# A planner's lengths for VectorE's work and the start of joined blocks, in a retention and feed-forward kernel

## The chip, the cores and the metric

The kernel runs on one core of a Trainium2 chip. The metric is the time of one execution in device microseconds (us). All runs told here were in the fast state or single looks of unknown state; the granted clock of TensorE was 0.997 to 1.0 in every run. Medians are of several runs. A ratio is the mean time of one kernel's fast runs over the mean of the other's fast runs of the same rounds, so it is not quite the ratio of the medians quoted.

## The reference, cut to what matters

Retention (attention with a decay in place of softmax) over 8 batches of 8 heads, 576 positions, head size 64; then a feed-forward layer whose activation is the squared relu. Everything is float32 outside; the kernel works in float16 with float32 sums.

```python
scores = scale * np.matmul(q, k.transpose(0, 1, 3, 2))
Dmat = np.where(rel >= 0, gamma[:, None, None] ** rel[None, :, :], 0.0)
attn = np.matmul(scores * Dmat[None], v)
x = attn.transpose(0, 2, 1, 3).reshape(B * S, H * D)     # 4608 x 512
r = np.maximum(x @ w_in, 0.0)                            # w_in 512 x 2048
out = (r * r) @ w_out                                    # w_out 2048 x 512
```

## The kernel before

The 4608 rows are 36 units of 128 rows, two to a group, 18 groups. A group goes through these steps:

- GpSimd casts k and q to float16 and multiplies v by its decay (units from 8 on); DMA transposes k and q.
- TensorE makes scores and sums of k and v in 64x64 tiles; VectorE masks the scores (rT), updates the states (Rm, stmp, R), and, after TensorE's outputs (psO), scales them into xT.
- TensorE multiplies xT by w_in (ph, first layer). ScalarE takes the relu (rl); the square (gT) is ScalarE's for seven of eight blocks and VectorE's for the last (from group 2 to 15; elsewhere VectorE has more of them).
- From group 2 on the second layer is a Strassen product: seven products in place of eight, for which VectorE first makes four sums and differences (gS), each in two halves. They are S1 to S4; S2 = gT(1,1) - S3 is used by the third product; its second half needs the last square, and S1, S4 follow.

The order on each engine isn't written by hand. Every piece is a task with an engine, a priority, a planned length in us and dependences. A list scheduler plays them through once, while the program is built, and each engine's instructions are emitted in the order so found:

```python
class Schedule:
    def add(self, eng, key, dur, fn, deps=(), acq=(), ...): ...
    def emit(self):
        ...        # at each moment each idle engine takes the ready task with the lowest key
        push(now + t["dur"], "end", t)
        ...
        for t in order:
            t["fn"]()
```

The chip then runs each engine's list in that order, waiting where a semaphore says so. A planned length that is wrong costs nothing in itself; it can put an instruction of TensorE ahead of something that isn't ready.

The other thing that the change touches is the joining. A group that isn't joined has a block fa (scores and sums) and later a block fb (outputs, in two parts with an explicit drain instruction of TensorE between). From group JOIN on, the outputs of a group and the scores and sums of the next are issued together, in f1 and f2, with no drain:

```python
def joined(g):
    return JOIN <= g < last_g
...
    def f1():
        emit_out1(g)
        emit_scores(g + 1)
    def f2():
        emit_sums(g + 1, "prS")
        emit_out2(g)
    ...                      # masks after f1; xT of g and the states of g + 1 after f2
else:
    def fb():
        emit_out1(g)
        nc.tensor.drain()
        emit_out2(g)
```

After f2, VectorE's keys put the first unit's xT, then the three state steps of the next group's first unit, then the second unit's xT. The next group's first layer needs both xT.

## Time and profile before

| | |
|---|---|
| time, median of 3 runs | 294.85 us (294.26 to 295.28) |
| the profiled execution | span 293.8 us, in a run of 295.6 us |
| TensorE busy | 284.2 us of the span |
| VectorE, ScalarE, GpSimd busy | 197.1, 188.0, 88.5 us |

The pages and lists that carry the argument stand in the prediction. One more view belongs beside them: busy time by engine in two stretches, where the column after the stretch is its length, then each engine's busy us and its count of instructions.

```profile
100.00:125.00 25.00, 23.46 (x420) 19.89 (x418) 18.88 (x37) 17.12 (x32) 8.49 (x10) 1.00 0.88 185
125.00:145.00 20.00, 19.19 (x291) 16.65 (x290) 14.22 (x29) 12.19 (x24) 8.66 (x11) 1.00 0.94 199
```

The order of the columns is TensorE matmul, TensorE weight load, VectorE, ScalarE, GpSimd. TensorE, busy nearly everywhere else, is idle for 1.54 us of the first stretch and 0.81 of the second.

### The profile page before, as it was taken

To read this page: it belongs to the slowest core of one execution; us is meant where nothing else is said; L and a number is where in the kernel's file an instruction comes from. 1 tells how busy PE (TensorE), PEld (TensorE's weight loads), DVE (VectorE), ACT (ScalarE), POOL (GpSimd) and SP (SyncE) were. 2 spreads that over 40 slices of the span, in tenths; PEclk is the share of its full clock that TensorE was granted. 3 is DMA by queue.
4 is the path that set the end of the run, shared out by engine and by line. 5 is a ranking of instruction groups with operands and counts; after the bars stand their busy time and mean duration, and the time that the engine had idled before them with its cause. 6 is when DMAs were issued, how large, how long until landed. Compare 5 with 4: busy or idle time off the path is not lost.

```text
span 293.8 us, 10069 instructions
## 1 busy us (share of the span) xinstructions
PE 284.2 (97%) x4328; PEld 234.0 (80%) x4328; DVE 197.1 (67%) x430; ACT 188.0 (64%) x354; POOL 88.5 (30%) x123
## 2 busy tenths in 40 slices
PE   8989999999999998999899999999999999999995
PEld 3548755688888877888788888888888888888884
DVE  3796579759484877757776867657796776564732
ACT  5457875386748665657576666766766576757830
POOL 4343364433343425151604142615150500000000
PEclk9999999999999999999999999999999999999999
DMA  7999999999989999797859599999796920201004
GB/s 201 327 370 386 366 286 266 217 230 191 232 203 194 183 198 199 177 201 184 179 144 211 139 199 208 204 212 184 187 192 163 165 74 2 74 3 71 2 0 145
DMA packets 139421, 54.14 MB, mean 184 GB/s; under 512 B 118128, under 2 KB 130928, under 8 KB 139376
## 3 DMA queue, kind: packets, MB, share of 16 engines
q1 hardware_dynamic: 139072, 53.23, 80.3%
q8 instruction: 34, 0.56, 0.9%
q10 hardware_dynamic: 304, 0.26, 0.3%
q14 instruction: 11, 0.09, 0.1%
HBM read 36.70 MB, written 9.44 MB: 157 GB/s over the span
## 4 chain that ended last, share of the span: by engine, by line
PE 85%; DVE 9%; ACT 3%; issue 1%; DVEq 0%
PE ph L827 38%; PE po L916 31%; PE po L865 5%; PE psO L343 4%; PE warm L247 3%; DVE gS L893 2%; PE psS L343 2%; PE psc L343 2%; PE psT L418 1%; ACT gT L845 1%; ACT rl L835 1%; DVE gT L847 1%; DVE xT L704 1%; DVE rx L461 1%; DVE vx L399 1%
## 5 line engine op out<-in xcount | busy, mean ns | idle before, releaser
L827 PE MATMUL ph<-xT,w_in 128*128 128x256 f16 x1152 | 138.3, 273 | 1.0 <-DVE xT L704 1.0
L827 PEld LDWEIGHTS <-w_in 128*128 128x128 f16 x1152 | 111.0, 98 | 15.8 <-DVE xT L704 1.2
L835 ACT ACTIVATE rl<-ph 128x512 f16<-128x512 f32 x144 | 84.2, 588 | 47.8 <-PE ph L827 44.0
L845 ACT ACTIVATE gT<-rl 128x512 f16<-128x512 f16 x104 | 65.6, 631 | 3.1
L916 PEld LDWEIGHTS <-gS 128*128 128x128 f16 x512 | 49.1, 98 | 8.4 <-DVE gS L893 2.3
L916 PE MATMUL po<-wT,gS 128*128 128x256 f16 x384 | 52.0, 273 | 1.5 <-DVE gS L893 1.5
L893 DVE TENSOR_TENSOR gS<-gT,gS 128x512 f16<-128x512 f16 x64 | 35.5, 556 | 13.3 <-ACT gT L845 12.7
L893 DVE TENSOR_TENSOR gS<-gT 128x512 f16<-128x512 f16 x64 | 31.2, 488 | 14.8 <-ACT gT L845 14.7
L916 PEld LDWEIGHTS <-gT 128*128 128x128 f16 x384 | 37.1, 98 | 4.5
L355 POOL CAST kq<-k 128x512 f16<-128x512 f32 x28 | 18.6, 666 | 63.2 <-DMA k<-in_k_dram 61.4
L916 PE MATMUL po<-w_out,gT 128*128 128x256 f16 x256 | 34.5, 273 | 0.0
L367 POOL TENSOR_TENSOR v<-v,vdec_full 128x512 f16<-128x512 f32 x24 | 26.0, 1084 | 20.4 <-DMA v<-in_v_dram 14.0
L847 DVE TENSOR_TENSOR gT<-rl 128x512 f16<-128x512 f16 x40 | 20.4, 509 | 15.3 <-ACT rl L835 15.0
L929 ACT COPY u<-po 128x256 f32<-128x256 f32 x32 | 11.9, 371 | 25.0 <-PE po L916 24.8
L355 POOL CAST kq<-q 128x512 f16<-128x512 f32 x28 | 18.7, 669 | 28.5 <-DMA q<-in_q_dram 28.3
L704 DVE TENSOR_TENSOR xT<-psO,gam_full 128x512 f16<-128x512 f32 x28 | 19.0, 686 | 8.2 <-PE psO L343 8.2
L939 DVE TENSOR_TENSOR o<-po,u 128x256 f32<-128x256 f32 x31 | 13.0, 421 | 15.5 <-ACT u L929 7.9
L643 DVE TENSOR_TENSOR rT<-psc,mask 128x512 f16<-128x512 f32 x28 | 18.2, 682 | 1.8 <-PE psc L343 1.6
L939 DVE TENSOR_TENSOR o<-po,p 128x256 f32<-128x256 f32 x17 | 7.2, 424 | 14.3 <-ACT u L929 8.0
L916 PE MATMUL po<-wT,gT 128*128 128x256 f16 x128 | 16.8, 273 | 0.0
L916 PE MATMUL po<-w_out,gS 128*128 128x256 f16 x128 | 16.8, 273 | 0.0
L865 PE MATMUL po<-w_out,gT 128*128 128x512 f16 x64 | 15.8, 380 | 0.0
(81 smaller groups left out, 245.0 us busy)
## 6 DMA issues: line engine op xcount, KB each, us to landing
out_dram<-o SPq DMA_DIRECT2D x31, 256.0 KB, 2.8
k<-in_k_dram SPq DMA_DIRECT2D x24, 256.0 KB, 4.6
q<-in_q_dram SPq DMA_DIRECT2D x24, 256.0 KB, 4.9
v<-in_v_dram SPq DMA_DIRECT2D x24, 256.0 KB, 4.6
wi<-in_moe_w_in_dram SPq DMA_DIRECT2D x4, 1024.0 KB, 9.8
wo<-in_moe_w_out_dram SPq DMA_DIRECT2D x4, 1024.0 KB, 9.6
pair<-in_k_dram SPq DMA_DIRECT2D x4, 512.0 KB, 7.1
pair<-in_q_dram SPq DMA_DIRECT2D x4, 512.0 KB, 7.3
```

The lines of the kernel that those rows point to most:

```text
L343: nc.tensor.matmul(out_, lhsT=lhsT, rhs=rhs, start=start, stop=True, skip_group_check=True, tile_position=(64 * row, 64 * col))
L355: op(out=out_.rearrange("p (n b a d) -> p n b a d", n=2, b=2, a=2), in_=in_.rearrange("p (n a b) d -> p n b a d", n=2, a=2))
L367: nc.gpsimd.tensor_tensor(out=t, in0=tile_of["v32", u], in1=vdec[kind].rearrange("p (h o) -> p h o", o=1).to_broadcast([P, H, D]), op=ALU. ...
L704: nc.vector.tensor_tensor(out=tile_of["x", g][:, :, s * P:(s + 1) * P].rearrange("p n (c i) -> p c n i", c=2), in0=tile_of["psO", g][:, :, ...
L827: nc.tensor.matmul(tile_of["ph", g, fb][:, j, :], lhsT=w_in16[:, m, fi * P:(fi + 1) * P], rhs=tile_of["x", g][:, m, :], start=(m == 0), st ...
L835: nc.scalar.activation(out=t, in_=tile_of["ph", g, fb], func=ACTF.Relu)
L845: nc.scalar.activation(out=t, in_=rl, func=ACTF.Square)
L847: nc.vector.tensor_tensor(out=t, in0=rl, in1=rl, op=ALU.mult)
L865: nc.tensor.matmul(tile_of["po", u], lhsT=tile_of["g", g][:, fi, s * P:(s + 1) * P], rhs=w_out16[:, fi, :], start=(fi == 0), stop=(fi == N ...
L893: nc.vector.tensor_tensor(out=Sx(k, h), in0=in0(h), in1=in1(h), op=op)
L916: nc.tensor.matmul(tile_of["pb", g, bank], lhsT=left(i), rhs=right[:, i, :], start=(start and i == 0), stop=(i == HF - 1), skip_group_chec ...
L939: nc.vector.tensor_tensor(out=o_tile(u)[:, half * HM:(half + 1) * HM], in0=bank(x), in1=tile_of[name, g], op=ALU.add)
```

## The change

The change plans VectorE's sums, states and squares longer than before, and lets the joining start one group later. No computing instruction is added or removed; group 6, no longer joined, gets a block with a drain of TensorE, which is new. The whole diff:

```diff
-    JOIN = 6
+    JOIN = 7
@@ states of the first groups
-            chain.append(add("DVE", base + 5.6 + s, 0.42, fr2, ...
+            chain.append(add("DVE", base + 5.6 + s, 0.5, fr2, ...
@@ states of the others
-            r2 = add("DVE", key + 0.3 + s, 0.35, fr2, ...
+            r2 = add("DVE", key + 0.3 + s, 0.5, fr2, ...
@@ squares
-            sq.append(add("ACT" if on_act else "DVE", place(4 * fb + 6), 0.63 if on_act else 0.45, fg, ...
+            sq.append(add("ACT" if on_act else "DVE", place(4 * fb + 6), 0.63 if on_act else 0.55, fg, ...
@@ sums of the Strassen products
-                out_.append(add("DVE", key + h, 0.45, f, deps=deps(h)))
+                out_.append(add("DVE", key + h, 0.55, f, deps=deps(h)))
```

More of the change, by code (lines that the diff above doesn't have):

```diff
@@ L495, in add_ret_pair @@
                 sched.free("ff", chain[-1:])
-            chain.append(add("DVE", base + 5.6 + s, 0.42, fr2, deps=[t] + chain[-1:], acq=("R",)))
+            chain.append(add("DVE", base + 5.6 + s, 0.5, fr2, deps=[t] + chain[-1:], acq=("R",)))
             if src is None:
@@ L679, in after_sums @@
             r1 = add("DVE", key + 0.2 + s, 0.42, fr1, deps=[r0])
-            r2 = add("DVE", key + 0.3 + s, 0.35, fr2, deps=[r1], acq=("R",))
+            r2 = add("DVE", key + 0.3 + s, 0.5, fr2, deps=[r1], acq=("R",))
             chain += [r0, r1, r2]
@@ L849, in add_ff @@
             sched.free("ff", [r])
-            sq.append(add("ACT" if on_act else "DVE", place(4 * fb + 6), 0.63 if on_act else 0.45, fg, deps=[r] + sq[:1],
+            sq.append(add("ACT" if on_act else "DVE", place(4 * fb + 6), 0.63 if on_act else 0.55, fg, deps=[r] + sq[:1],
                           acq=() if fb else ("g",)))
```

## The prediction

> **What bounds the kernel now.** I read the first page first, then the list of who waited for whom, then the timeline of each place where TensorE waited.
>
> ```profile
> PE 284.2 (97%) x4328; PEld 234.0 (80%) x4328; DVE 197.1 (67%) x430; ACT 188.0 (64%) x354; POOL 88.5 (30%) x123
> PEclk9999999999999999999999999999999999999999
> PE 85%; DVE 9%; ACT 3%; issue 1%; DVEq 0%
> ```
>
> TensorE is busy for 284.2 of 293.8 us, its clock is granted in full, and 85% of the chain that ended last is its own work. Because matmul ends are modelled, I checked the pace by starts: in the chain 20 matmuls of 128x256 take 2.18 us, so 0.109 us each, from end to end of the trace. The change keeps every matmul, so it can only win back time in which TensorE stood still, or lose more of it. The list of waits says how much that is:
>
> ```profile
> PE po L916 <- DVE gS L893: 1.5, 3, 0.8
> PE warm L247 <- DVE junk L163: 1.3, 1, 1.3
> PE ph L827 <- DVE xT L704: 1.0, 1, 1.0
> PE psO L343 <- DVE R L489: 0.9, 1, 0.9
> PE psS L343 <- DVE vx L399: 0.3, 1, 0.3
> PE psS L343 <- DVE rT L643: 0.2, 1, 0.2
> ```
>
> All of TensorE's waits are for VectorE and they are few. Warm-up, R L489 and vx lie in the first 23 us, where the order hardly changes. The rest can be reached: sums of the Strassen products (gS), the scaled retention output (xT), the masks (rT). Two of these places follow each other (start, length, then the group):
>
> ```profile
> 108.53 1.47 PE L916 MATMUL po<-wT,gS 128*128 128x256 f16 x12
> 110.97 2.36 PE L827 MATMUL ph<-xT,w_in 128*128 128x256 f16 x20 [0.96 <-DVE xT L704]
> 113.71 0.61 PE L916 MATMUL po<-wT,gS 128*128 128x256 f16 x4 [0.39 <-DVE gS L893]
> ```
>
> Twelve matmuls from 108.53 should let the next start at 108.53 + 12 x 0.109 = 109.84; it starts at 110.97, so 1.13 us are lost. Twenty from 110.97 should end at 113.15; the next is at 113.71, so 0.56 us. The same sum at two more places: four matmuls from 141.72, next at 143.13, 0.97 us; four from 230.36, next at 231.25, 0.45 us. Before the masks, twelve from 119.58, next at 121.23, 0.34 us, of which 0.09 is the usual changeover to small tiles. Together 1.13 + 0.56 + 0.97 + 0.45 + 0.25 = 3.36 us. From 145 to 222 us TensorE is busy 76.91 of 77 us. What made VectorE late at 142:
>
> ```profile
> 139.85 0.42 DVE L893 TENSOR_TENSOR gS<-gT,gS 128x512 f16<-128x512 f16 x1
> 140.18 0.83 DVE L893 TENSOR_TENSOR gS<-gT 128x512 f16<-128x512 f16 x1
> 140.93 0.83 DVE L847 TENSOR_TENSOR gT<-rl 128x512 f16<-128x512 f16 x1
> 141.79 1.27 DVE L893 TENSOR_TENSOR gS<-gT,gS 128x512 f16<-128x512 f16 x1
> ```
>
> One shape of sum takes 0.42, 0.83 or 1.27 us. GpSimd ran a cast of q from 140.83 and v's product from 141.75, for 1.04 us. 26 of the 128 sums and 8 of the 40 squares are over 0.5 us; means are 488 and 556 ns for the two kinds of sum and 509 ns for the squares, where the kernel's own planner counts 450. Its states (L672) take 0.42 us all but once, against 0.35 planned.
>
> **What the Trainium skill says.** "TensorE: Matmul & The Clock Gate", Back-to-back issue gap, gives N/2.4 + 2.5 ns, 109.2 ns for 256 columns; the trace agrees (0.109). "GPSIMD Engine Reference", Specifications, says that its SBUF interfaces are shared with VectorE, with contention for instructions "with two SBUF inputs". The trace agrees: sums have two such inputs and stretch, while xT (678 to 693 ns) and the masks (674 to 693 ns), which read PSUM, do not. "TensorEngine Tiling (Array Packing)", Key Properties, says that changing the tiling mode drains TensorE; the trace shows some 0.09 us extra at each changeover, and their number stays.
>
> **The change part by part.** The kernel simulates its engines once and emits each one's instructions in the order so found. The durations are planning numbers: no instruction is added or removed, only order moves. I counted it in the built programs. GpSimd's order is the same task by task; DMA differs in some stores and loads that swap places.
>
> First, JOIN from 6 to 7. The work runs in groups 0 to 17 of two units. From JOIN on, a group's retention outputs are issued in the same blocks as the next group's scores and sums. Before, group 6 was joined and came late: between the end of its outputs and the first matmul that needs its xT, TensorE has 20 matmuls, 2.18 us, whereas VectorE has xT, three state steps and xT again: 2 x 0.69 + 3 x 0.44 = 2.7 us, with two sums still queued ahead. That is the wait of 1.13, and what VectorE then still owed makes the 0.56. After, group 6 stands alone: 60 matmuls (6.55) and a block of scores and sums (0.78) lie between, 7.3 us against 1.4 us of VectorE. Both waits go: 1.69 us won. The price is one more block with an explicit drain in it: in group 5's block the small matmuls start at 85.84 and then at 86.14, where neighbours are 0.01 to 0.02 apart; 0.28 us.
>
> Second, the longer sums. At group 7 the critical sum is the second half of S2, used by the third product. Before, from the outputs of group 8, TensorE has 60 matmuls to that use (6.55) and VectorE 6.63 us nominal work; with stretched sums it was 0.97 late. After, TensorE has 64 (6.98), and one sum (0.52) stands ahead of the xT steps, so VectorE has 6.11. The slack grows by 0.95 us, just the wait. I leave 0.2. Group 13's wait at 230 hangs on the last square: from the last first-layer matmul to the use there were 32 matmuls (3.49), now 36 (3.93): 0.44 of the 0.45 gone, I leave 0.05. For groups 8 to 11 the same distance grows by 0.44 to 1.31 us, for 12 not at all.
>
> Third, where slack shrinks. xT of groups 7, 8, 9 came 1.19, 1.62 and 2.46 us early; the distance falls by 0.44, 0.44 and 1.31, leaving 0.75 to 1.2 us. One stretched sum costs up to 0.85, so I put 0.1. The masks keep 2.18 us of TensorE work, for groups 12 and 13 it falls to that from 3.49 and 2.62, against 1.4 us of VectorE plus a sum; the old 0.25 stays and 0.15 is added.
>
> Sum: won 3.36 - 0.25 - 0.2 - 0.05 = 2.86; lost 0.28 + 0.1 + 0.15 = 0.53; net 2.3 us. 294.85 - 2.3 = 292.5 us.
>
> **The rivals.** One: the waits move rather than vanish. Stretching depends on which sum meets which cast, and GpSimd runs when DMA lands, so a new order draws new lots; when I match each sum's end with the start of the matmul that uses it, five S2 halves (groups 5, 7, 8, 12, 13) came within 0.06 us of need or late. For it: that thin margin, and group 12 unchanged. Against it: smallest planned slack rises from -0.16 to about 0.9 us among groups 7 to 9. It would give back 1 to 2 us: 293.5 to 294.5. Two: first-layer matmuls move forward between products, three accumulators are then held of four PSUM buffers, and ScalarE's relu and square (0.59 + 0.63 = 1.22 us against 0.87 us of four pairs of matmuls) become the wait. For it: in groups 7 to 9 five first-layer blocks in place of two now stand among the first products. Against it: TensorE never waits for ScalarE in the list above, and ScalarE is 64% busy. It would give about 293.5 to 295. Three: all reachable waits vanish, masks too: 294.85 - 3.36 + 0.28 = 291.8. A gain over 2% (below 289) would need more than TensorE's waits hold; a loss over 2% would need 6 us of new waits.
>
> **Range and chances.** Between rival three less run-to-run spread (0.5 us) and rival one: 291.3 to 294.4. Same within 2% is nearly certain: 0.965; faster 0.02, slower 0.015.
>
> **What would show it.** Right: the wait for xT is gone from TensorE's list, that for gS falls from 1.5 to under 0.5 us, TensorE's busy time stays at 284 us, its idle time between 100 and 145 us falls by about 2.5 us, one more small gap of 0.28 in a retention block, and sums still stretched in some 30 cases. Wrong: new gS or xT waits at groups 7 to 12, a wait for rl L835, or a gap in the first 60 us, where a few blocks of scores and outputs swapped with neighbours.

## The result, and the profile after

The changed kernel took 292.81 us (median of 4 runs, 292.64 to 292.98), the kernel before 294.56 us beside it (4 runs, 293.81 to 295.28). The ratio is 0.9941, 95% interval 0.9913 to 0.9968: faster by 0.6%, within the 2% that the verdict calls the same. The profiled execution spans 290.9 us.

The page's busy times and the chain that ended last, of the changed kernel:

```profile
PE 283.0 (97%) x4328; PEld 234.0 (80%) x4328; DVE 195.0 (67%) x430; ACT 187.5 (64%) x354; POOL 88.9 (31%) x123
PE 89%; DMA 6%; SPq 1%; issue 1%; POOL 1%; DVE 0%; DVEq 0%; POOLq 0%
```

VectorE's 9% of the chain is gone. The chain is now TensorE's own work, traced back to the first loads (DMA 6%). The list of TensorE's waits says the same:

```profile
PE warm L247 <- DVE junk L163: 1.3, 1, 1.3
PE psO L343 <- DVE R L489: 0.9, 1, 0.9
PE psT L418 <- DVE qx L403: 0.4, 1, 0.4
PE psS L343 <- DVE vx L399: 0.3, 1, 0.3
PE ph L827 <- POOL w_in L322: 0.2, 1, 0.2
```

All five lie in the first 28 us. The waits for gS, xT and rT are no longer listed. In the two stretches TensorE is now busy for all but 0.08 us:

```profile
100.00:125.00 25.00, 24.92 (x435) 21.64 (x433) 16.75 (x41) 17.82 (x34) 8.03 (x11) 1.00 1.01 191
125.00:145.00 20.00, 20.00 (x300) 17.61 (x299) 13.60 (x27) 13.89 (x27) 8.99 (x12) 1.00 0.93 198
```

What did not go is the stretching. VectorE's timeline of the changed kernel at the same group as before:

```profile
140.03 0.88 DVE L893 TENSOR_TENSOR gS<-gT,gS 128x512 f16<-128x512 f16 x1
140.83 0.41 DVE L893 TENSOR_TENSOR gS<-gT 128x512 f16<-128x512 f16 x1
141.17 2.01 DVE L893 TENSOR_TENSOR gS<-gT,gS 128x512 f16<-128x512 f16 x2
```

GpSimd's timeline shows what the first of them ran beside:

```profile
140.02 0.62 POOL L355 CAST kq<-q 128x512 f16<-128x512 f32 x1 [1.31 <-DMA q<-in_q_dram]
141.09 1.05 POOL L367 TENSOR_TENSOR v<-v,vdec_full 128x512 f16<-128x512 f32 x1 [0.46 <-DMA v<-in_v_dram]
```

The cast runs from 140.02 to 140.64. The sum began at 140.03 and ended at 140.91, 0.27 us after the cast. This is so throughout: in every trace of this case, each sum or square of VectorE over 0.5 us began while a GpSimd instruction was running and ended 0.27 to 0.28 us after that instruction's end (32 of 32 here, 34 of 34 in the kernel before). A stretched sum is thus not slowed by a share; it is held until GpSimd is done, so its length depends on how much of GpSimd's instruction was left.

The sum at 140.03 takes 0.88 us and ends at 140.91; it is the second half of S2 of group 7, the very sum that was 0.97 us late before. TensorE's timeline shows who was waiting for it:

```profile
138.88 1.47 PE L827 MATMUL ph<-xT,w_in 128*128 128x256 f16 x12
140.19 0.60 PE L916 MATMUL po<-wT,gS 128*128 128x256 f16 x4
140.62 1.47 PE L827 MATMUL ph<-xT,w_in 128*128 128x256 f16 x12
141.94 0.60 PE L916 MATMUL po<-wT,gS 128*128 128x256 f16 x4
```

Nobody: twelve matmuls of the first layer now stand between the two halves of the product, where four stood before, and the half that needs the sum starts at 141.94, 1.03 us after it is ready. In all, 29 sums and 3 squares of the changed kernel are over 0.5 us (26 and 8 before). The order makes room for them; it does not shorten them.

The price of the later joining is in the trace too: group 6's outputs are now a block with a drain, and the step across it, from the first part to the second, is plain (the last of the four matmuls of the first line starts at 101.74, so it is 0.28 us):

```profile
101.70 0.23 PE L343 MATMUL psO<-kqT,Rm 64*64 64x64 f16 x4
102.02 0.32 PE L343 MATMUL psO<-rT,v 64*64 64x64 f16 x16
```

How much TensorE gained as a whole is read from its last group of matmuls, the same in both kernels:

```profile
289.27 1.04 PE L916 MATMUL po<-wT,gT 128*128 128x256 f16 x8
```

```profile
286.06 1.04 PE L916 MATMUL po<-wT,gT 128*128 128x256 f16 x8
```

The first is of the kernel before, the second of the changed one: 3.21 us earlier. Of that, 0.13 us came before the first layer of group 0 began, which leaves 3.08. The span is only 2.9 us shorter. The missing 0.31 us lies behind all work: from the landing of the last store to the end of the program the kernel before takes 1.09 us and the changed one 1.41 (see the last section).

### The profile page after: what moved, and what is told of

It reads as the page before. It is cut to its first block, busy times and chain, and to the rows that moved or that the text cites. A ratio compares the mean times of both kernels' runs of the same rounds, so it can differ in the third digit from the quotient of the medians.

```text
span 290.9 us, 10062 instructions
## 1 busy us (share of the span) xinstructions
PE 283.0 (97%) x4328; PEld 234.0 (80%) x4328; DVE 195.0 (67%) x430; ACT 187.5 (64%) x354; POOL 88.9 (31%) x123
## 4 chain that ended last, share of the span: by engine, by line
PE 89%; DMA 6%; SPq 1%; issue 1%; POOL 1%; DVE 0%; DVEq 0%; POOLq 0%
PE ph L827 42%; PE po L916 34%; PE po L865 5%; PE psO L343 4%; DMA wi<-in_moe_w_in_dram 3%; DMA pair<-in_q_dram 3%; PE psc L343 2%; PE psS L343 2%; SPq L298 1%; POOL w_in L322 1%; PE psT L418 1%; DVE o L939 0%; POOL qx L403 0%; DVE p L968 0%; DVEq L939 0%
## 5 line engine op out<-in xcount | busy, mean ns | idle before, releaser
L847 DVE TENSOR_TENSOR gT<-rl 128x512 f16<-128x512 f16 x40 | 18.9, 473 | 14.7 <-ACT rl L835 14.2
```

Of the source, the lines that this page charges most:

```text
L847: nc.vector.tensor_tensor(out=t, in0=rl, in1=rl, op=ALU.mult)
```

## The experiments

Twelve runs follow, in three calls; within a call all ran on one chip, beside the kernel before. The calls were on different chips, so a comparison across calls is the weaker one; there the ratio to the kernel before is the safer number. The theory: TensorE's waits come where the planned order leaves VectorE's work too little time; the planner's longer lengths and the later joining make that slack, and the stretched sums decide how much of a missing slack is felt. The slack is counted from the built orders, with 0.109 us for a matmul and the usual durations of VectorE's steps: TensorE's work between a group's outputs and the use, less VectorE's work in the same span. It ignores what is queued ahead. Where it is negative, VectorE is late by plan. "By starts" below means a loss read from the starts of two matmuls that follow each other, less 0.109 us; it is larger than the wait in the list, since matmul ends are modelled.

| kernel | xT of first joined group | second half of S2 (used by the third product) of groups 6, 7, 8, 9, 10 | TensorE's work between last first-layer matmul and that use, groups 10, 11, 12, 13 |
|---|---|---|---|
| before | -0.5 (group 6) | -0.1, -0.1, -0.2, 0.3, 1.6 | 3.9, 3.5, 3.9, 3.5 |
| joining only | 0.3 (group 7) | 0.0, 0.0, 0.4, -0.2, 0.3 | 3.5, 3.9, 3.5, 3.9 |
| lengths only | -0.5 (group 6) | 0.8, 0.8, 0.7, 1.1, 1.1 | 3.9, 3.9, 3.9, 4.2 |
| joining and states | 0.8 (group 7) | 0.5, 0.4, 0.4, 0.9, 0.3 | 3.5, 3.5, 3.9, 3.5 |
| joining and sums | 0.8 (group 7) | 0.5, 0.4, 0.4, 0.9, 0.7 | 3.9, 3.9, 3.9, 3.9 |
| the change | 0.8 (group 7) | 0.9, 0.9, 0.9, 0.9, 1.3 | 4.4, 3.9, 3.9, 3.9 |

### The joining alone

```diff
-    JOIN = 6
+    JOIN = 7
```

> Only the joining is moved from group 6 to group 7; the planner keeps the old lengths. Theory (planned slack decides): group 6's xT wait of 1.1 us and the 0.56 us behind it go, one block with a drain (0.28 us) is added, but in this order the third product's second half of S2 has no planned slack in groups 6 and 7 (0.0 us) and 9 (-0.2), so waits for gS of 0.3 to 1 us remain in one to three places: about 293.5 us, and its runs spread by more than 0.5 us. Rival (the joining is all of the gain): 292.8 as the whole change, ratio 0.994, no gS wait.

Measured: 293.52 us (12 runs, 292.72 to 294.34), before 294.94 (23 runs, 293.9 to 295.9), ratio 0.9952 (0.9937 to 0.9967). As the theory had it. The runs spread over 1.6 us, and the wait left in the trace is for a sum:

```profile
PE po L916 <- DVE gS L893: 0.3, 1, 0.3
```

It came in group 12, not in 6, 7 or 9 as I had counted; those had 0.37 to 0.60 us to spare in this run. A count of slack says where a wait can come, not where it comes in one run.

### The lengths alone

```diff
 (the change, but)
+    JOIN = 6
```

> Only the planner's lengths are changed; group 6 stays joined. Theory: group 6's xT still comes late by about 1 us (planned slack -0.5 us before queued sums), perhaps with a gS wait behind it (planned slack -0.3), while S2's halves of groups 6 to 13 all have 0.7 us or more of planned slack, so no gS wait after 115 us: about 293.5 us. Rival (the lengths are all of the gain): 292.8, no wait for xT.

Measured: 293.62 us (12 runs, 293.3 to 294.4), ratio 0.9958 (0.9946 to 0.9971). The wait that planning cannot see away with group 6 joined is there:

```profile
PE ph L827 <- DVE xT L704: 0.6, 1, 0.6
```

By starts 0.80 us are lost there and 0.28 us at the sum behind it, in place of 1.13 and 0.56. No wait for gS is listed. So each half of the change gives 1.3 to 1.4 us and both together 1.8 to 2.3: they overlap, since the lengths already soften the late group 6.

### Both kernels again

> The kernel before once more, for a second trace. Theory: the xT wait at group 6 comes again at 1.0 to 1.2 us since it is planned short; the gS waits come at other sizes (between 0 and 1 us each) since they are drawn anew; total idle of TensorE differs from the first trace by as much as the run's time does. The first trace was of a run of 295.6 us, slower than the median 294.56, so the reachable 3.36 us are probably 0.5 to 1 us less here. Rival: the same waits at the same sizes.

> The changed kernel once more. Theory: ratio 0.994 (292.8 us), runs within 0.5 us of each other, since no wait for VectorE is left after the first 25 us; the kernel before, timed beside it, spreads over 1 us or more, since its waits hang on which sum meets which GpSimd instruction. Rival (the spread is the chip's): both spread alike.

The kernel before was looked at once more (one run, 295.66 us). Its list of waits for VectorE in the region in question:

```profile
PE ph L827 <- DVE xT L704: 1.0, 1, 1.0
PE po L916 <- DVE gS L893: 0.8, 3, 0.4
...
PE psS L343 <- DVE rT L643: 0.3, 1, 0.3
```

Much comes back at its place: by starts 1.14 us for xT and 0.45 behind it (1.13 and 0.56 in the first trace), 0.44 before the masks (0.34) and 0.52 in group 13 (0.45). The 0.97 us at group 7 did not come, and others of 0.26 (group 12) and 0.35 (at 67 us) did. So I was right about xT, but only part of the gS waits is drawn anew. I had expected 0.5 to 1 us less in total because the first trace was of a slow run; this run was as slow, so that part was not tested. The changed kernel took 292.67 us (6 runs, 292.44 to 293.04) and its runs spread over 0.6 us, those of the kernel before over 2.0 us. The spread belongs to the kernel, not to the chip. The changed kernel's second trace has one wait for gS of 0.2 us (0.32 by starts), in group 12, where the change gave no slack.

### GpSimd that reads nothing

The k and q casts and v's product from group 4 on become stores of a constant on GpSimd, in the same order. The result is wrong on purpose.

```diff
-            sorted_cast(nc.gpsimd.tensor_copy, t[:, 0], tile_of["k32", u])
+            nc.gpsimd.memset(t[:, 0], 0.01)
 (q and v alike)
```

> The kernel before in its own order, but from group 4 on GpSimd writes a constant where it cast k and q and scaled v: it reads nothing from SBUF (a wrong result, on purpose). Theory (sums are stretched by GpSimd's reads, and the scattered waits come of that): hardly any sum or square from 50 us on is over 0.5 us; the waits for gS and rT shrink to 0.3 us in sum; the wait for xT at group 6 stays near 1 us, since it is short by plan; some 293.5 us, 1.0 to 1.4 less than before. Rival (DMA traffic stretches the sums, or the order alone makes the waits): stretched sums as many as before, waits and time as before.

> The same edit on the changed kernel. Theory: nothing to win, since its slack already covers the stretched sums: 292.5 us, within 0.4 us of the changed kernel, no wait for VectorE after 25 us. Rival (stretched sums still cost the changed kernel time): 291.5 or less.

Measured: the kernel before 292.59 us (4 runs, 292.51 to 292.89; ratio 0.9917), the changed kernel 292.40 us (4 runs, 292.32 to 292.54; ratio 0.9909). The two kinds of sum in the quiet kernel before (count, then busy us and mean ns):

```profile
L893 DVE TENSOR_TENSOR gS<-gT 128x512 f16<-128x512 f16 x64 | 26.9, 420 | 15.5 <-ACT gT L845 15.4
L893 DVE TENSOR_TENSOR gS<-gT,gS 128x512 f16<-128x512 f16 x64 | 26.9, 421 | 13.7 <-ACT gT L845 13.1
```

Not one of 128 sums is over 0.5 us, against 26, and GpSimd still writes all those tiles: it is its reads, not its writes, that stretch them. Of these sums 11 ran at the same time as such a store (17 in the quiet version of the changed kernel), and none took over 0.43 us. And the old order alone, unstretched, is as good as the new one with stretching: TensorE's last group starts at 286.27 us. I had expected 293.5 us and was 0.9 us too high, because I took the xT wait of group 6 to be planned and so to stay near 1 us. It falls to 0.4 us listed (0.59 by starts): the other half was stretched sums queued ahead of xT. All waits for gS and rT are gone, so the scattered ones were contention altogether. The spread goes with them: 0.4 us over 4 runs, where the kernel before, beside it, spread over 1.8 us in 11. For the changed kernel the edit wins 0.2 to 0.4 us against medians from other calls, and its closing after the last landing is 0.32 us shorter here (1.09 for 1.41), so little of that can be VectorE's.

### Joining one group later still

```diff
-    JOIN = 7
+    JOIN = 8
```

> The changed kernel with the joining started one group later still, at 8. Theory: no wait left to remove, so only the price shows: one more block with a drain, a step of 0.25 to 0.28 us inside group 7's outputs, time 0.2 to 0.3 us longer than the changed kernel, 292.9 to 293.1. Rival (later joining goes on helping through slack of xT): 292.4 or less.

Measured: 293.08 us (6 runs, 292.75 to 293.18), ratio 0.9929 (0.9913 to 0.9945), no wait for gS or xT. It is 0.3 to 0.5 us above the medians of the changed kernel, from other calls; by the ratio to the kernel before it can't be told from the changed kernel (0.9925 to 0.9941). So the price isn't shown in the time. The step itself is in the trace of group 7's outputs:

```profile
116.71 0.19 PE L343 MATMUL psO<-kqT,R 64*64 64x64 f16 x1
117.00 0.32 PE L343 MATMUL psO<-rT,v 64*64 64x64 f16 x16
```

From 116.71 to 117.00 it is 0.29 us, where neighbours are 0.00 to 0.05 apart.

### Which of the lengths

```diff
 e11: JOIN = 7, and of the lengths only
-            r2 = add("DVE", key + 0.3 + s, 0.35, fr2, ...
+            r2 = add("DVE", key + 0.3 + s, 0.5, fr2, ...          (and 0.42 to 0.5 in the first groups)
 e12: JOIN = 7, and of the lengths only
-                out_.append(add("DVE", key + h, 0.45, f, deps=deps(h)))
+                out_.append(add("DVE", key + h, 0.55, f, deps=deps(h)))
```

> Joining from 7, and of the lengths only the states' 0.50 us; measured they take 0.42, so this plan is made wrong on purpose of the change, not right. Theory (any length planned longer gives slack, true or not): planned slack of the critical half of S2 rises from 0.0 to 0.5 us in groups 6 and 7.. and -0.2 to 0.9 in group 9, but stays at 0.3 to 0.7 in groups 10 and 13: between joining alone and all of it, 292.9 to 293.3, with a gS wait of 0.1 to 0.5 us in group 12 or 13. Rival (only the true lengths help): 293.5, as joining alone.

> Joining from 7, and of the lengths only the sums' 0.55 us. Theory: planned slack 0.4 to 0.5 us in groups 6 to 8, 0.7 to 1.1 from 9 on, and at least 3.9 us of TensorE work behind the last square but for group 6: 292.8 to 293.1, nearly the whole change, a gS wait of at most 0.3 us. Rival (the three lengths add up in equal parts): 293.2.

> The changed kernel beside the three others on one chip: 292.6 to 292.9, ratio 0.992 to 0.994 to the kernel before; runs within 0.6 us.

On one chip, beside the kernel before at 294.38 us (14 runs): joining and states 293.47 us (9 runs, 292.89 to 293.97; ratio 0.9969, 0.9953 to 0.9985), joining and sums 292.83 us (6 runs, 292.71 to 293.13; ratio 0.9942), the whole change 292.59 us (6 runs, 292.43 to 292.99; ratio 0.9933). The sums' length does nearly all of the lengths' work. The states' does nothing that shows beyond the joining (293.52 us and a ratio of 0.9952, in another call), though I had counted 0.4 us or so more slack for groups 6 to 9 and expected 292.9 to 293.3. The time is that of the rival, that only true lengths help: the states take 0.42 us and were planned at 0.50, while the sums' 0.55 is near their mean of 0.49 to 0.56. Another reading is the last column of the table, which the states' length leaves at 3.5 us in groups 10, 11 and 13. Its one look, the fastest of its nine runs, has a loss of 0.27 us by starts before a sum in group 11. That this column is what binds fits both rows, but it isn't shown: no run varied it alone, and the changed kernel itself lost 0.32 us in group 12 with 3.9 us there. Squares alone weren't run.

### Longer still, and xT first

```diff
 e9: the change, and
-            ... 0.63 if on_act else 0.55, fg, ...
+            ... 0.63 if on_act else 0.7, fg, ...
-                out_.append(add("DVE", key + h, 0.55, f, deps=deps(h)))
+                out_.append(add("DVE", key + h, 0.7, f, deps=deps(h)))
 e10: e9, and
+    JOIN = 6
-            T["x", u] = add("DVE", key + at, 0.7, fx, ...
+            T["x", u] = add("DVE", key + 0.3 * at, 0.7, fx, ...
```

> The changed kernel planned with sums and squares at 0.70 us instead of 0.55. By plan every group's critical half of S2 then has 1.3 us of slack or more from group 6 on (0.9 in the changed kernel), and the last square at least 4.4 us of TensorE work before its use (3.9). Theory: the last waits for gS of 0.2 to 0.3 us in groups 12 and 13 go, worth 0 to 0.3 us: 292.4 to 292.7, spread under 0.6 us. Rival (longer plan lengths push first-layer blocks against the four PSUM buffers and ScalarE): 293 or more, with a wait for rl.

> A version to beat both: joining from group 6 again (one drain less), sums and squares planned at 0.70 us, and VectorE does a group's second xT straight after the first, ahead of the state steps (1.3 us earlier). By plan xT of group 6 then has 1.2 us of slack (-0.5 in the kernel before), and every critical half of S2 1.0 us or more. Theory: no wait for xT or gS above 0.3 us, and the drain's 0.25 us gained on the changed kernel: 292.3 to 292.5, 0.2 to 0.4 less than the changed kernel beside it. Rival (stretched sums queued ahead of xT still make group 6 late, as in the kernel before): an xT wait of 0.3 us or more and 292.7 or more.

Planned at 0.70: 292.80 us (6 runs, 292.36 to 292.86; ratio 0.9917), no wait for gS or rl listed. It is no better and no worse than the change as far as these runs tell: once the waits are gone, more planned slack buys nothing that shows. I had expected 292.4 to 292.7.

With xT first: 292.85 us (6 runs, 292.69 to 293.17; ratio 0.9941), where the change beside it took 292.59; I had expected it to be 0.2 to 0.4 us faster. It does on TensorE what it was meant to: joining at group 6 costs no xT wait (0.25 us by starts are lost at 112.3 to a relu of ScalarE that frees its PSUM buffer at 112.59, too little for the list), and its last group of matmuls starts earlier than the changed kernel's in the same call:

```profile
286.26 1.04 PE L916 MATMUL po<-wT,gT 128*128 128x256 f16 x8
```

```profile
285.89 1.04 PE L916 MATMUL po<-wT,gT 128*128 128x256 f16 x8
```

The first is of the change, the second of this version: 0.37 us. All of it is lost afterwards: from the start of the last matmul to the last store's landing 2.96 us in place of 2.68, and from there to the end 1.52 in place of 1.41. Both spans are 291.1 us. Why the last stores land later I didn't settle. No correct version that ran beats the change beyond the noise.

## Why the prediction was right, point by point

The predicted time was 292.5 us in a range of 291.3 to 294.4; the first measurement was 292.81, the two later ones 292.67 and 292.59. A gain of 2.3 us was forecast; the medians give 1.75, 2.27 and 1.79 us.

- **What bounds it.** Right. TensorE's chain share went from 85% to 89%, VectorE's from 9% to 0. "TensorE: Matmul & The Clock Gate", Back-to-back issue gap, gives the formula that I quoted for an isolated gap, not for a stream of weight loads and matmuls as here; that this stream keeps to it (0.109 us) is shown by the trace.
- **First part, group 6.** Right. Both waits went with the joining alone. Half of the 1.13 us was, however, not the planned shortage but a stretched sum queued ahead of xT (1.26 us from 106.53): with GpSimd's reads away it is 0.59.
- **The drain, 0.28 us.** Right: from start to start 0.28 us in the change's new block, and 0.29 us in the one after when group 7 got it too.
- **Second part, the sums.** Right in kind. The second half of S2 of group 7 came 0.83 to 1.03 us ahead of its use in three traces of the change, where 0.97 us had been lost. Groups 12 and 13 stayed tight: in each of these traces at least one of the two came within 0.06 us of its use.
- **Third part, xT.** Predicted 0.75 us and 1.2 us to spare for groups 7 and 8, and 1.15 for group 9; measured 0.76, 1.19 and 1.21 in the first trace of the change. No wait came, for which 0.1 us had been put.
- **Masks.** The 0.25 us that I left and the 0.15 that I added did not come in any trace of the change. The mask wait was stretching as well: it is gone in the quiet kernel before, whose order is the old one.
- **Rivals.** The first, waits that move rather than vanish, was right only for a remnant in group 12 (0.2 us listed in one of three traces). The second, ScalarE and the PSUM buffers, did not occur: no list of waits names rl. The third, 291.8 us, is what TensorE did (3.21 us earlier), yet not what the clock showed.

The gain is off by 0.03 to 0.55 us, and three terms account for it, of opposite signs; that they nearly cancel, and 292.5 came so close, is partly luck. The waits left over, 0.75 us in my sum with the masks, were hardly there: on TensorE the trace shows 3.21 us won, 3.08 of it after the first layer began, which is 3.36 - 0.28 = 3.08, as if every wait had gone. Against that, the 3.36 us was read from one trace of a run of 295.6 us, and was taken as every run's: the second look too was of a slow run, and the kernel before had medians of 294.4 to 294.9. With spreads of up to 2 us, a typical run must lose about 1 us less than the traced ones; this follows from the times and was not traced in a typical run. And 0.31 us come back after the last store has landed, which nothing in the order foretold.

## What to carry to other kernels

Where one engine is bound and its order is fixed ahead of time, look for the few places where it waits, count the work between cause and use on both engines, and give the fixed order slack there; here planning the unsteady sums at 0.55 us in place of 0.45 did most of what the lengths did. Planning the steady states too long did nothing that shows, and 0.70 us did no more than 0.55; look at which tasks a length moves before trusting it. Before sizing a gain by one trace, compare the traced run's time with the median: where waits hang in part on contention, one run is one draw. Check also what lies behind the last useful instruction, since a gain of a few tenths of a us can end there.

## What the Trainium skill lacked or had wrong

- "GPSIMD Engine Reference", Specifications, has the shared SBUF interfaces and the contention with instructions of two SBUF inputs, but not its size. "SBUF — State Buffer" has more: such an instruction contends with a GpSimd instruction that reads SBUF, not with one that only writes it (Who interferes with whom), and whichever starts second is blocked for the whole of the other (SBUF: two separate sides). The traces agree: when GpSimd only writes (a memset of the same tiles, 0.53 us each), no sum is over 0.5 us, and a held sum ends just after GpSimd's instruction. What neither page has is how long after: 0.27 to 0.28 us, every time, for a 128x512 float16 sum that takes 0.42 us undisturbed and up to 1.30 us when held. Of 128 sums 26 to 35 are over 0.5 us in the traces where GpSimd reads.
- "TensorEngine Tiling (Array Packing)", Key Properties, says that changing the tiling mode drains TensorE, without a figure: some 0.09 us extra at each change to small tiles here. An explicit drain between two parts of 64x64 outputs shows as 0.27 to 0.29 us from start to start.
- No page has the closing steps that a program itself issues (in the trace they carry line 1051 of kernel.py). From the last store's landing to the end takes 1.08 or 1.09 us in four of the fourteen traces and 1.38 to 1.54 us in ten. It is the same in every trace of one kernel (1.09 twice for the kernel before, 1.41 three times for the change). In those ten, and in no other, GpSimd's closing steps are late and an 8,192-byte packet of an instruction queue (q14) starts 1.6 to 2.1 us after the landing, which is after the program's end. Why they are late is open; no run tested it.
